# A fused linear-attention and mixer block: a lone row-tile pair for the last two tiles, and another order of all jobs

## The chip, the cores and the metric

The kernel runs on one core of one Trainium2 chip. The metric is the device time of one execution in microseconds (us), less is better. "TensorE" or PE is the matmul engine (PEld are its weight loads), DVE is VectorE, ACT is ScalarE, POOL is GpSimd, SP is SyncE, which here only issues DMAs.

## The reference

All tensors are bfloat16. x has 2048 tokens of 448 features; there are 16 heads of 28 features; w3 and w4 have 1792 hidden features.

```python
def _A_ref(x, wqkv, w_phi, wo):                 # linear attention
    q, k, v = heads(x @ wqkv)                   # 16 heads of 28
    pq, pk = q @ w_phi, k @ w_phi               # per head
    phi_q = concat(softmax(pq), softmax(-pq))   # 56 features a head
    phi_k = concat(softmax(pk), softmax(-pk))
    kv, z = phi_k^T v, sum_s phi_k
    o = (phi_q kv) / (phi_q z + 1e-6)
    return o.reshape(B, S, D) @ wo

def _B_ref(x, w1, w2, w3, w4):                  # token-shift mixer and MLP
    h = gelu(layernorm(x) @ w1)
    hs = concat(h[..., quarter i] shifted by (+1, -1, +2, -2)[i] tokens) @ w2
    x1 = x + hs
    return x1 + gelu(layernorm(x1) @ w3) @ w4

x = A_x
xn = layernorm(x)
return x + _A_ref(xn, A_wqkv, A_w_phi, A_wo) + _B_ref(xn, B_w1, B_w2, B_w3, B_w4)
```

## The kernel before

The 2048 tokens are 16 tiles of 128. A recorder (`Recorder`) takes every instruction in program order, works out which earlier ones it must wait for, and writes one instruction stream for each engine; each engine then runs its stream strictly in order. So the order in which the program calls its jobs is the order on every engine and on SP's DMA queue. Nearly all instructions are issued through helpers, which is why the profile's lines repeat: L204 is every matmul, L208 every transposing matmul, L212 every activation, L216 every elementwise operation of DVE and POOL, L219 a transposing DMA, L222 a plain DMA.

**Row pairs.** 448 rows of a contraction are held as four overlapping chunks of 128 rows that start at rows 0, 128, 192 and 320 (`load_lap`, `START`). Each chunk has a lower half (partitions 0 to 63, `LO`) and an upper half (64 to 127, `HI`). Rows 192 to 255 stand twice, so a product over 448 rows is seven halves. Two matmuls of 64 rows, one on each half and into different PSUM banks, run side by side in TensorE. For two tiles together 14 halves make seven such pairs. The recorder's rule: two matmuls that write the same PSUM bank from different halves are ordered by a semaphore wait (`solve`, lines 114 to 121). There are eight banks of 512 fp32 columns.

**First stage** (a list of jobs that `chain` plays, lines 969 to 990). It loads x, makes the layernorm statistics (`m` on DVE; the root as a power on POOL, `r`, or on ACT, `q`; the apply on DVE, `a`, or POOL, `p`), transposes each normalised tile into `xnT` (`XT` on TensorE with a copy out by ACT or DVE, or `XD` as a DMA on SP), computes V (`ZV`, copied out by `EV`), h = gelu(xn w1) (`ZH`, `ZW`, and `ZR` for the last 64 features; gelus by `EW` and `rest_out` on ACT), and folds w_phi into the q and k weights (`FO`). `HD` issues dummy matmuls into idle time. `chain` keeps one list of lower and one of upper halves and interleaves them: an upper half is issued `lag` columns after the lower half of the same bank. `h_shift` makes the token shift of h as six SBUF-to-SBUF DMAs per half of the tokens, `rest_T` transposes the gelu's last 64 features by DMA (tile `hR`, which shares its memory with `gT`, into `hRT`); both are on SP's queue.

**Second stage** (the list in `play`, lines 1055 to 1077). Its jobs: `k0`, `k1` and `q0`, `q1` (k and q features of two tiles in four and three row pairs of 448 columns, then two exponentials on ACT), `w0`, `w1_` (h w2 of two tiles, also four and three pairs; two adds on DVE bring the sum into `xn`, `w2_out`), `kn` (sums for k's softmax: a reduce and a reciprocal on DVE), `kx` (their product on POOL), `T` (transpose of q's exponentials by DMA), `K` (phi_k^T v of a tile into banks 6 and 7, eight pairs of 59 columns), `kc`, `kb` (kv to SBUF), `lo`, `sc` (statistics of the second norm), `A` (its apply, on POOL or DVE), `G` (its transpose by DMA into `gT`), `a`, `b` (w3 for 256 hidden features of 512 tokens, in four and three row pairs of 512 columns, then a gelu on ACT), `N` (numerator and denominator of a tile, six DVE operations, two on POOL, then the transpose `o_T` by DMA), `f` (four steps over a pair of tiles: w4 and wo into banks 4 and 5, then `fin_out` on DVE), `S` (store).

Which banks k, q, w2, V and h jobs use is fixed in `kq`, `wb`, `vb` and `gb`.

**The last two tiles.** Tiles 14 and 15 have no partner pair behind which their tail could hide, so they use 128-row matmuls: 14 of w4 and four of wo each. Since rows 192 to 255 stand in two chunks, `num_tile` fills 64 of the attention output's columns with zeros for these tiles. Tile 14 is one matmul group of 448 columns (`fin_full`), tile 15 is two groups of 256 and 192 columns (`fin_split`), each with its own add and store, the first store on ACT's queue and the last on SP's.

Of the kernel before, what the change touches and what calls it, by code (L numbers as in the profile page):

```python
# [18 lines left out]
class Recorder:  # L19
# [56 lines left out]
    def solve(self):  # L76
# [10 lines left out]
        for eng, fn, w, r, dma, tile in self.ops:  # L87
# [137 lines left out]
def bass_parallel_sum__linear_kernel_hedgehog__mixer_s_mlp__prompt_kernel(  # L225
# [17 lines left out]
    with es:  # L243
# [533 lines left out]
        def num_tile(i):  # L777
# [54 lines left out]
        def fin_bank(i):  # L832
            return (0 if i > 13 else 4) + i % 2

        def fin_full(i):
            g, j = divmod(i, 4)
            b = banks[fin_bank(i)]
            x_sum(i)
            for fc in range(FC):
                R.mm(b[:, 0:D], h3T[:, g % 2, fc, 128 * j:128 * j + 128], w4[:, fc, :], fc == 0, False)  # L840
            for kc in range(KC):
                R.mm(b[:, 0:D], oT[:, g % 2, kc, 128 * j:128 * j + 128], wo[:, kc, :], False, kc == KC - 1)

        def fin_split(i, cut):
            g, j = divmod(i, 4)
            x_sum(i)
            for n, (c0, c1) in enumerate(((0, cut), (cut, D))):
                b, c = banks[2 * n + 1], slice(c0, c1)
                for fc in range(FC):
                    R.mm(b[:, c], h3T[:, g % 2, fc, 128 * j:128 * j + 128], w4[:, fc, c], fc == 0, False)  # L850
                for kc in range(KC):
                    R.mm(b[:, c], oT[:, g % 2, kc, 128 * j:128 * j + 128], wo[:, kc, c], False, kc == KC - 1)
                R.ew(dve, "tensor_tensor", outb[:, i % 4, c], b[:, c], xs[:, i % 2, c], op=ALU.add)
                R.dma(out2d[128 * i:128 * i + 128, c], outb[:, i % 4, c], "SP" if n else "ACT")
# [59 lines left out]
        fb = {(1, 0): 3, (1, 2): 1, (0, 0): 3, (0, 2): 1}  # L914
# [4 lines left out]
        def L(*ops):  # L919
            return do(ln1, *ops)  # L920
# [39 lines left out]
        def HF(p, n):  # L960
# [4 lines left out]
        vb = {0: 2, 1: 5, 2: 4, 3: 6, 4: 5, 5: 4, 6: 6, 7: 7, 8: 0, 9: 7, 10: 1, 11: 4, 12: 7, 13: 0, 14: 5, 15: 3}  # L965
        gb = ((7, 2, 3), (1, 7, 0), (1, 0, 3), (4, 5, 6))
# [3 lines left out]
            HD(3, 3), HD(3, 3), do(load_wT, 0, (1, 2, 3)), L(("m", 0)), HD(6, 3), L(("r", 0, 1), ("a", 0), ("v", 1)),  # L970
            HD(2, 3), L(("m", 2), ("q", 1, 1), ("m", 3)), XT(0, 2, 1, "ACT"),
            L(("p", 1), ("q", 2, 1), ("a", 2), ("r", 3, 1), ("m", 5), ("m", 4), ("p", 3)), HD(4, 3), HD(5, 3),
            inside(3, ZV(0, EV(0, "ACT", 1)), XT(1, 5, 1, "ACT")), XT(2, 0, 1, "ACT"), ZV(1, EV(1, "ACT", 1)),
            L(("q", 5, 1)), inside(1, ZV(2, EV(2, "ACT", 1)), XT(3, 0, 1, "ACT")),
            L(("m", 6), ("q", 6, 1), ("p", 5), ("q", 4, 1), ("m", 7)), ZH(2, 0), L(("a", 6), ("a", 4)),
            inside(2, ZH(0, 0), XT(5, 0, 1, "ACT")), L(("r", 7, 1), ("m", 12), ("p", 7)), ZH(0, 1, EW(0, 0, 1)), ZH(1, 0),
            XT(6, 0, 1, "DVE"), XT(4, 5, 1, "ACT"), ZH(2, 1), L(("m", 13)), ZV(5, EV(5, "ACT", 1)), L(("r", 12, 1)),
            XT(7, 0, 1, "DVE"), L(("m", 14), ("p", 12), ("r", 13, 1)), ZV(4, EV(4, "ACT", 1)), ZV(3, EV(3, "ACT", 1)),
            L(("m", 15), ("r", 14, 1), ("m", 8)), ZH(1, 1, EW(0, 1, 2)), ZW(1, 1, EW(1, 1, 1)), ZW(1, 2, EW(1, 2, 1)),
            L(("r", 15, 1)), XT(12, 4, 1, "ACT"), ZV(6, EV(6, "ACT", 1)), L(("a", 14), ("a", 15), ("a", 13)), do(load_w2),  # L980
            XT(14, 2, 2, "2"), inside(2, ZW(1, 0, EW(1, 0, 1)), XT(13, 4, 1, "DVE")), L(("r", 8, 1), ("p", 8)),
            ZV(7, EV(7, "ACT", 1)), L(("m", 10)), ZW(3, 0, EW(3, 0, 1)), L(("m", 11)), ZV(15, EV(15, "ACT", 1)),
            L(("r", 10, 1)), XD(8), L(("p", 10), ("m", 9), ("r", 11, 1)), XD(10), ZV(14, EV(14, "ACT", 1)), do(phi_blocks),
            ZV(13, EV(13, "ACT", 1)), L(("a", 11)), XD(11), L(("r", 9, 1)), FO(1, 2, 0), do(load_w3, 0),
            inside(2, ZW(3, 2, EW(3, 2, 1)), FO(1, 2, 1)), inside(2, ZV(12, EV(12, "ACT", 1)), FO(1, 0, 0)), FO(1, 0, 1),
            do(h_shift, 0), ZW(3, 1, EW(3, 1, 1)), inside(1, ZV(8, EV(8, "ACT", 1)), FO(0, 2, 0)), L(("p", 9)),
            XT(9, 3, 1, "DVE"), FO(0, 2, 1), ZR(0, 6, (rest_out, 0, 6), (rest_T, 0)), ZV(9, EV(9, "ACT", 1)), do(late_3),
            FO(0, 0, 0), ZV(10, EV(10, "ACT", 1)), inside(1, ZR(1, 2, (rest_out, 1, 2)), FO(0, 0, 1)), ZW(2, 1, EW(2, 1, 1)),
            ZV(11, EV(11, "ACT", 1)), ZW(2, 2, EW(2, 2, 1)), ZW(2, 0, EW(2, 0, 1)), HF(2, 0), HF(0, 0), do(load_w4),
            do(kv_picks), do(h_shift, 1), HF(1, 0), do(kv_ones), do(rest_T, 1), HF(0, 1), HF(1, 1), HF(2, 1)], 500, 2)  # L990

        on_dve = (7, 8, 12, 13, 15)
# [58 lines left out]
        def wo_in(eng="SP"):  # L1051
# [4 lines left out]
            (k0, 1), (kn, 0), (w0, 2), (k1, 1), (k0, 2), (T, 0), (kx, 0), (lo, 1), (w1_, 2), (kn, 1), (k1, 2), (q0, 1),  # L1056
            (q0, 2), (q1, 1), (kn, 2), (q1, 2), (w0, 4), (k0, 3), (w1_, 4), (T, 1), (k1, 3), (kx, 1), (q0, 3), (k0, 4),
            (q1, 3), (k1, 4), (w0, 6), (T, 2), (kn, 3), (lo, 2), (q0, 4), (w1_, 6), (kx, 2), (kx, 3), (T, 4), (K, 0), (K, 3),
            (q1, 4), (lo, 0), (K, 5), (T, 3), (T, 7), (T, 6), (lo, 3), (sc, 0), (k0, 5), (K, 4), (A, 1), (kn, 4), (A, 3),
            (k1, 5), (q0, 5), (T, 5), (A, 2), (A, 0), (load_w3, 1), (G, 1), (w0, 8), (G, 3), (q1, 5), (k0, 6), (w1_, 8),  # L1060
            (k1, 6), (K, 2), (q0, 6), (kn, 5), (w0, 10), (q1, 6), (w1_, 10), (G, 2), (lo, 7), (kx, 4), (lo, 5), (lo, 4),
            (G, 0), (k0, 7), (lo, 6), (K, 7), (kn, 6), (kx, 5), (K, 6), (k1, 7), (q0, 7), (w0, 12), (q1, 7), (w1_, 12),
            (sc, 4), (a, 0), (A, 6), (A, 4), (kx, 6), (G, 6), (kn, 7), (K, 1), (K, 10), (b, 0), (a, 1), (K, 9), (lo, 10),
            (K, 11), (wo_in,), (K, 8), (b, 1), (w0, 14), (G, 4), (a, 2), (a, 3), (b, 2), (b, 3), (A, 7), (lo, 11), (A, 5),
            (lo, 8), (kx, 7), (w1_, 14), (G, 5), (K, 13), (a, 4), (G, 7), (T, 12), (lo, 9), (a, 5), (b, 4), (K, 12), (T, 14),
            (K, 15), (sc, 8), (K, 14), (kc,), (b, 5), (lo, 12), (a, 6), (kb,), (A, 10), (b, 6), (a, 7), (N, 1), (b, 7),
            (f, 1, 0), (N, 0), (T, 10), (A, 11), (G, 10), (a, 8), (a, 9), (A, 8), (T, 11), (G, 8), (A, 9), (b, 8), (b, 9),
# [13 lines left out]
        fin_split(15, 256)  # L1081
# [30 lines left out]
```

## Time and profile before

| | us |
|---|---|
| median of 3 runs | 173.25 |
| the three runs | 173.14, 173.25, 176.32 |
| the profiled execution's own time | 172.24 |
| its span, first to last instruction | 170.5 |
| TensorE busy in the span | 166.2 |
| DVE, POOL, ACT busy | 108.4, 92.2, 83.9 |

"Busy" is the time in which at least one instruction of the engine runs. The span is one execution; the time around it is not in the trace. In the timeline rows, the columns are the start and the length in us, the engine, the line, the operation, what it writes and reads, the shapes, the number of instructions merged, and in brackets the idle time before it with what ended it. Where matmuls are merged, the length includes the last one's way through the array, so a pitch is read from start to start. The granted TensorE clock was full throughout.

### The profile page before, as it was taken

The page shows a single profiled execution, that of the slowest core. Times are in us where ns is not written, and L with a number is a line of the kernel's source. Part 1 is how long each engine was busy: PE and PEld are TensorE (multiplying, and loading weights), DVE is VectorE, ACT ScalarE, POOL GpSimd, SP SyncE. Part 2 cuts the span into 40 slices and gives each one's busy share as a digit, 9 for nine tenths or more (in the row PEclk, how much of TensorE's full clock was granted, in tenths as well). Part 3 has the DMA queues.
Part 4 walks back from the last instruction along what each step waited for, and adds up shares of the span by engine and source line. Part 5 has one row for each costly group of instructions (what it writes and reads, how often), then busy time and mean ns, then how long its engine had stood idle before and what let it go on. Part 6 is the DMA issues. An engine that isn't in the chain of part 4 may idle for free.

```text
span 170.5 us, 5420 instructions
## 1 busy us (share of the span) xinstructions
PE 166.2 (97%) x2351; PEld 96.3 (56%) x2351; DVE 108.4 (64%) x246; ACT 83.9 (49%) x114; POOL 92.2 (54%) x128
## 2 busy tenths in 40 slices
PE   8899999999999999999999999999999999999994
PEld 7576789655555555554554554554545555545463
DVE  3798865249999799967678933757407552425621
ACT  5789866879999879357242240421304222404000
POOL 6588590005799999992585272094420754023740
PEclk9999999999999999999999999999999999999999
DMA  5995677999599940569037949945440113021141
GB/s 153 359 207 99 150 84 210 190 351 171 118 134 191 257 98 0 142 126 94 0 64 136 113 96 168 139 105 78 92 115 0 35 31 112 4 58 31 31 117 48
DMA packets 51111, 20.07 MB, mean 118 GB/s; under 512 B 42256, under 2 KB 50384, under 8 KB 51088
## 3 DMA queue, kind: packets, MB, share of 16 engines
q1 hardware_dynamic: 49968, 18.86, 58.1%
q10 hardware_dynamic: 1120, 0.87, 1.5%
q8 instruction: 18, 0.29, 0.8%
q14 instruction: 5, 0.04, 0.1%
HBM read 7.14 MB, written 1.84 MB: 53 GB/s over the span
## 4 chain that ended last, share of the span: by engine, by line
PE 88%; DMA 5%; SPq 3%; DVE 1%; POOL 1%; issue 1%
PE banks L204 87%; SPq L222 3%; DMA hRT<-gT 2%; DMA xtok<-in_A_x_dram 2%; PE banks L208 1%; DVE st L216 1%; POOL rs L216 0%; POOL xn L216 0%; DVE xnT L216 0%; DVE mv L216 0%; DVE vaug L216 0%
## 5 line engine op out<-in xcount | busy, mean ns | idle before, releaser
L212 ACT ACTIVATE phik<-banks 128x1024 bf16<-128x1024 f32 (+1 forms) x44 | 41.8, 985 | 61.1 <-PE banks L204 61.0
L204 PE MATMUL banks<-gT,w 64*128 64x512 bf16 x392 | 48.0, 376 | 0.0
L216 DVE TENSOR_TENSOR vaug<-banks,vaug 128x464 f32<-128x464 f32 (+3 forms) x65 | 32.7, 513 | 23.1 <-PE banks L204 21.4
L204 PE MATMUL banks<-w,phik 64*128 64x448 bf16 (+3 forms) x434 | 45.2, 343 | 0.0
L216 POOL TENSOR_TENSOR xnT<-vaug 128x280 bf16<-128x280 f32 (+1 forms) x32 | 18.1, 586 | 45.9 <-DVE vaug L216 45.9
L204 PEld LDWEIGHTS banks<-w,phik 64*128 64x128 bf16 (+1 forms) x434 | 22.8, 94 | 19.1 <-issue 0.4
L204 PE MATMUL banks<-wv,xnT 64*128 64x448 bf16 (+3 forms) x222 | 32.4, 346 | 0.2
L734 POOL TENSOR_TENSOR phik<-phik,rks 128x1792 bf16<-128x1792 bf16 x8 | 25.6, 3212 | 9.1 <-DVE rks L216 8.8
L204 PEld LDWEIGHTS banks<-gT,w 64*128 64x128 bf16 x392 | 18.0, 94 | 18.4 <-ACT phik L212 0.7
L204 PEld LDWEIGHTS banks<-wv,xnT 64*128 64x128 bf16 (+1 forms) x222 | 14.0, 94 | 8.1 <-ACT xnT L212 0.8
L216 POOL TENSOR_TENSOR vaug<-xn,xtok 128x448 f32<-128x448 bf16 x16 | 16.2, 1031 | 1.1 <-DVE vaug L216 1.1
L216 DVE TENSOR_REDUCE ksum<-phik 128x64 f32<-128x1792 bf16 x8 | 16.0, 1996 | 0.2 <-ACT phik L212 0.2
L204 PE MATMUL banks<-xnT,w 64*128 64x512 bf16 (+1 forms) x105 | 16.0, 334 | 0.0
L212 ACT ACTIVATE hi<-banks 128x896 bf16<-128x896 f32 x16 | 13.7, 919 | 2.3 <-PE banks L204 2.3
L204 PE MATMUL banks<-wpk,xnT 64*128 64x448 bf16 x112 | 14.2, 349 | 0.0
L204 PE MATMUL banks<-wpq,xnT 64*128 64x448 bf16 x112 | 13.7, 349 | 0.0
L216 DVE RECIPROCAL vaug<-banks 128x16 f32<-128x16 f32 x16 | 4.1, 254 | 15.2 <-PE banks L204 15.2
L216 POOL TENSOR_TENSOR rs<-mv,mhalf 128x1 f32<-128x1 f32 (+1 forms) x15 | 10.4, 697 | 5.3 <-DVE mv L216 5.2
L204 PE MATMUL banks<-w,hT 64*128 64x448 bf16 x96 | 12.8, 349 | 0.0
L216 DVE TENSOR_TENSOR xn<-banks,xn 128x512 bf16<-128x512 f32 (+1 forms) x16 | 9.0, 601 | 3.6 <-PE banks L204 3.6
L216 DVE BATCH_NORM_STATS2 st<-xn 128x6 f32<-128x448 bf16 x16 | 9.4, 590 | 0.0
L216 DVE BATCH_NORM_STATS2 st<-xtok 128x6 f32<-128x448 bf16 x15 | 9.0, 601 | 0.4 <-DMA xtok<-in_A_x_dram 0.4
(71 smaller groups left out, 167.2 us busy)
## 6 DMA issues: line engine op xcount, KB each, us to landing
w<-in_B_w_dram SPq DMA_DIRECT2D x2, 896.0 KB, 5.7
out_dram<-vaug SPq DMA_DIRECT2D x15, 112.0 KB, 1.9
w<-in_B_w_dram SPq DMA_DIRECT2D x1, 1568.0 KB, 9.3
xtok<-in_A_x_dram SPq DMA_DIRECT2D x2, 448.0 KB, 6.3
wv<-in_A_wo_dram SPq DMA_DIRECT2D x2, 224.0 KB, 3.8
xtok<-in_A_x_dram SPq DMA_DIRECT2D x3, 112.0 KB, 3.9
xtok<-in_A_x_dram ACTq DMA_DIRECT2D x3, 112.0 KB, 4.1
w<-in_B_w_dram SPq DMA_DIRECT2D x1, 336.0 KB, 4.4
```

Of the source, the lines that this page charges most:

```text
L204: self.op("PE", lambda e: e.matmul(out, lhsT, rhs, start=start, stop=stop, skip_group_check=True), [out], [lhsT, rhs], tile=self._tile(lhsT))
L208: self.op("PE", lambda e: e.transpose(out, in_, ident), [out], [in_, ident], tile=self._tile(in_))
L212: self.op("ACT", lambda e: e.activation(out, in_, func, **kw), [out], [in_] + aps)
L216: self.op(eng, lambda e: getattr(e, name)(out, *args, **kw), [out], aps)
L222: self.op(eng, lambda e: e.dma_start(out, in_), [out], [in_], dma=True)
L734: R.op(pool, lambda e: e.tensor_tensor(ph, ph, wide, op=ALU.mult), [ph], [ph, wide, *after])
```

## The change

It does these things.

1. The recorder's rule is widened: a wait is also set where the same half wrote the same bank before a change between 64-row and 128-row form.
2. `fin_tails` is new. Chunk 1's lower half (rows 128 to 191) for tile 14 and chunk 2's upper half (rows 256 to 319) for tile 15 are issued as a pair of 64 rows that opens the three output groups; the full matmuls that follow then need only three chunks a tile. The zero fill goes.
3. Tile 15's groups become 320 and 128 columns.
4. Tile 14's second norm apply moves from POOL to DVE (`on_dve` has six tiles now).
5. The first stage's list, its banks (`vb`, `gb`, `fb`), `lag` (500 to 300) and `even` (2 to 1) are others. Tile 8 is transposed on TensorE and no longer by DMA, tile 3's root goes to ACT, V of tiles 3 and 8 is copied out by DVE, and several of the copies out of `XT` change between ACT and DVE.
6. The second stage's list has the same 259 entries in another order. Banks of k, q, w2 and w3 jobs stay.

```diff
-                        if lo != tile[0]:
+                        if lo != tile[0] or m != mode[1]:
...
-            if i >= NT - 2:
-                c0 = 192 + 64 * (i % 2)
-                R.ew(pool, "memset", o_tok[:, i % 4, c0:c0 + 64], 0.0)
...
+        def fin_tails(i, cut):
+            x_sum(i)
+            g, j = divmod(i, 4)
+            c = 128 * j
+            R.mm(banks[0][:, 0:D], oT[0:64, g % 2, 1, c:c + 128], wo[0:64, 1, :], True, False)
+            for n, (c0, c1) in enumerate(((0, cut), (cut, D))):
+                R.mm(banks[2 * n + 1][:, c0:c1], oT[64:128, g % 2, 2, c + 128:c + 256], wo[64:128, 2, c0:c1], True, False)
+
+        def fin_steps(b, i, c, kcs):
+            g, j = divmod(i, 4)
+            s = slice(128 * j, 128 * j + 128)
+            for fc in range(FC):
+                R.mm(b[:, c], h3T[:, g % 2, fc, s], w4[:, fc, c], False, False)
+            for kc in kcs:
+                R.mm(b[:, c], oT[:, g % 2, kc, s], wo[:, kc, c], False, kc == KC - 1)
+
         def fin_full(i):
-            g, j = divmod(i, 4)
-            b = banks[fin_bank(i)]
-            x_sum(i)
-            for fc in range(FC):
...
+            fin_steps(banks[0], i, slice(0, D), (0, 2, 3))
...
+                fin_steps(b, i, c, (0, 1, 3))
...
-            L(("m", 0)), HD(6, 3), L(("r", 0, 1), ("a", 0), ("v", 1)),
-            HD(2, 3), L(("m", 2), ("q", 1, 1), ("m", 3)), XT(0, 2, 1, "ACT"),
-            L(("p", 1), ("q", 2, 1), ("a", 2), ("r", 3, 1), ("m", 5), ("m", 4), ("p", 3)), HD(4, 3), HD(5, 3),
...
-            L(("r", 10, 1)), XD(8), L(("p", 10), ("m", 9), ("r", 11, 1)), XD(10), ZV(14, EV(14, "ACT", 1)), do(phi_blocks),
...
+            HD(1, 3), L(("m", 0), ("r", 0, 1), ("a", 0)), HD(2, 3), L(("v", 1), ("q", 1, 1), ("m", 2)), HD(0, 3),
+            XT(0, 6, 1, "ACT"), L(("p", 1), ("m", 3), ("q", 2, 1)), HD(1, 3), L(("q", 3, 1)), HD(3, 3),
+            L(("a", 2), ("m", 5)), HD(3, 3), inside(2, ZV(0, EV(0, "ACT", 1)), XT(1, 0, 1, "ACT")), L(("m", 4)),
+            XT(2, 6, 1, "ACT"), ZV(1, EV(1, "ACT", 1)), L(("m", 6), ("p", 3), ("q", 5, 1)), XT(3, 0, 1, "ACT"),
...
+            FO(1, 0, 1), L(("p", 9)), XT(8, 1, 1, "ACT"), ... inside(2, ZV(8, EV(8, "DVE", 1)), FO(0, 0, 0)), do(h_shift, 0),
...
-        on_dve = (7, 8, 12, 13, 15)
+        on_dve = (7, 8, 12, 13, 14, 15)
...
-            (G, 0), (k0, 7), (lo, 6), (K, 7), (kn, 6), (kx, 5), (K, 6), (k1, 7), (q0, 7), (w0, 12), (q1, 7), (w1_, 12),
-            (sc, 4), (a, 0), (A, 6), (A, 4), (kx, 6), (G, 6), (kn, 7), (K, 1), (K, 10), (b, 0), (a, 1), (K, 9), (lo, 10),
-            (K, 11), (wo_in,), (K, 8), (b, 1), (w0, 14), ...
+            (lo, 6), (G, 1), (K, 5), (kx, 5), (lo, 7), (K, 2), (k1, 7), (sc, 4), (w0, 12), (A, 5), (q0, 7), (A, 4),
+            (w1_, 12), (G, 4), (q1, 7), (K, 4), (a, 0), (kn, 6), (w0, 14), (b, 0), (a, 1), ...
...
-            (f, 3, 5), (a, 26), (f, 4, 5), (S, 10), (N, 14), (b, 27), (b, 26), (f, 1, 6), (f, 2, 6), (N, 15), (f, 3, 6),
-            (S, 11), (S, 12), (S, 13)])
+            (f, 4, 5), (a, 26), (S, 11), (S, 10), (N, 15), (S, 9), (a, 27), (b, 26), (b, 27), (f, 1, 6), (f, 2, 6),
+            (f, 3, 6), (S, 12), (S, 13)])
+        fin_tails(14, 320)
         fin_full(14)
         fin_out(14)
         store(14)
-        fin_split(15, 256)
+        fin_split(15, 320)
```

More of the change, by code (lines that the diff above doesn't have):

```diff
@@ L848, in fin_split @@
                 b, c = banks[2 * n + 1], slice(c0, c1)
[L849 to L852, printed above, removed]
+                fin_steps(b, i, c, (0, 1, 3))
                 R.ew(dve, "tensor_tensor", outb[:, i % 4, c], b[:, c], xs[:, i % 2, c], op=ALU.add)
@@ L912, in ln1 @@
                     ln1_apply(pool if op == "p" else dve, *n)
-        fb = {(1, 0): 3, (1, 2): 1, (0, 0): 3, (0, 2): 1}
+        fb = {(1, 0): 4, (1, 2): 1, (0, 0): 3, (0, 2): 3}
         def do(f, *args):
@@ L963, in HF @@
             return "half", halves_of(*head[p][n], n == 0), then
[L965 to L966 removed]
+        vb = {0: 5, 1: 3, 2: 4, 3: 6, 4: 5, 5: 4, 6: 6, 7: 5, 8: 0, 9: 1, 10: 7, 11: 5, 12: 7, 13: 0, 14: 2, 15: 7}
+        gb = ((7, 2, 3), (0, 7, 0), (0, 3, 1), (3, 5, 6))
         spin(30)
@@ L975, in bass_parallel_sum__linear_kernel_hedgehog__mixer_s_mlp__prompt_kernel @@
[L975 to L979, printed above, removed]
@@ L985, in bass_parallel_sum__linear_kernel_hedgehog__mixer_s_mlp__prompt_kernel @@
[L985 to L989, printed above, removed]
@@ new lines, in bass_parallel_sum__linear_kernel_hedgehog__mixer_s_mlp__prompt_kernel @@
+            L(("m", 7), ("q", 4, 1), ("p", 5)), ZH(1, 0), ZV(2, EV(2, "ACT", 1)), do(load_wT, 0, (1, 2, 3)),
+            L(("q", 6, 1), ("p", 4), ("a", 6)), ZH(0, 0), L(("m", 13)), XT(5, 0, 1, "ACT"), L(("r", 7, 1)),
+            ZH(0, 1, EW(0, 0, 1)), ZH(2, 0), L(("m", 12)), XT(4, 5, 1, "ACT"), XT(6, 0, 1, "ACT"), L(("m", 14), ("p", 7)),
+            ZH(2, 1), L(("r", 13, 1)), ZV(5, EV(5, "ACT", 1)), L(("r", 12, 1)), ZV(3, EV(3, "DVE", 1)), XT(7, 0, 1, "DVE"),
+            L(("r", 14, 1)), ZV(4, EV(4, "ACT", 1)), L(("m", 15)), ZH(1, 1, EW(0, 1, 2)), ZW(1, 2, EW(1, 2, 1)), do(load_w2),
@@ new lines, in bass_parallel_sum__linear_kernel_hedgehog__mixer_s_mlp__prompt_kernel @@
+            ZW(1, 1, EW(1, 1, 1)), L(("p", 13), ("a", 12), ("a", 14), ("r", 15, 1), ("a", 15)), XT(12, 4, 1, "DVE"),
+            L(("m", 10), ("r", 10, 1), ("m", 11)), ZV(6, EV(6, "ACT", 1)), L(("r", 11, 1), ("p", 10), ("m", 8)),
+            XT(14, 1, 2, "ACT"), XT(13, 3, 1, "DVE"), ZV(7, EV(7, "ACT", 1)), do(phi_blocks), L(("m", 9)),
+            ZW(1, 0, EW(1, 0, 1)), L(("r", 8, 1)), ZV(14, EV(14, "ACT", 1)), XD(10), L(("a", 8), ("a", 11), ("r", 9, 1)),
+            XD(11), ZV(15, EV(15, "ACT", 1)), do(load_w3, 0), ZW(3, 0, EW(3, 0, 1)),
@@ new lines, in bass_parallel_sum__linear_kernel_hedgehog__mixer_s_mlp__prompt_kernel @@
+            inside(2, ZV(13, EV(13, "ACT", 1)), FO(1, 0, 0)), FO(1, 0, 1), L(("p", 9)), XT(8, 1, 1, "ACT"),
+            ZW(3, 2, EW(3, 2, 1)), inside(2, ZV(12, EV(12, "ACT", 1)), FO(1, 2, 0)), do(late_3), XT(9, 3, 1, "DVE"),
+            FO(1, 2, 1), ZW(3, 1, EW(3, 1, 1)), inside(2, ZV(8, EV(8, "DVE", 1)), FO(0, 0, 0)), do(h_shift, 0), FO(0, 0, 1),
+            ZR(0, 6, (rest_out, 0, 6), (rest_T, 0)), ZV(9, EV(9, "ACT", 1)),
+            inside(2, ZR(1, 2, (rest_out, 1, 2)), FO(0, 2, 0)), ZW(2, 0, EW(2, 0, 1)), ZV(10, EV(10, "ACT", 1)), FO(0, 2, 1),
@@ L993, in bass_parallel_sum__linear_kernel_hedgehog__mixer_s_mlp__prompt_kernel @@
+            ZV(11, EV(11, "ACT", 1)), ZW(2, 2, EW(2, 2, 1)), ZW(2, 1, EW(2, 1, 1)), HF(0, 0), HF(2, 0), HF(1, 0),
+            do(kv_picks), do(load_w4), do(rest_T, 1), do(kv_ones), do(h_shift, 1), HF(0, 1), HF(1, 1), HF(2, 1)], 300, 1)
+        on_dve = (7, 8, 12, 13, 14, 15)
         kp = [phi_pair(wpk, 2 * n, kq[n][0]) for n in range(8)]
```

49 lines of the change are left out of this document (19 added, 30 removed).

## The prediction

> **What bounds the kernel now.** I read the page's busy shares first, then the busy time by stage, then who made TensorE wait, and only then the stretches that the new order touches.
>
> ```profile
> span 170.5 us, 5420 instructions
> PE 166.2 (97%) x2351; PEld 96.3 (56%) x2351; DVE 108.4 (64%) x246; ACT 83.9 (49%) x114; POOL 92.2 (54%) x128
> ```
> ```profile
> 9.12:34.24 25.12, 24.86 (x480) 19.33 (x480) 16.92 (x45) 20.50 (x38) 13.66 (x25) 1.00 0.85 152
> 34.24:68.00 33.76, 33.76 (x485) 18.61 (x486) 29.97 (x44) 29.26 (x35) 26.08 (x17) 1.00 0.85 166
> 68.00:161.04 93.04, 93.04 (x1246) 47.82 (x1238) 53.71 (x138) 28.42 (x30) 44.31 (x58) 1.00 0.46 81
> ```
> ```profile
> PE banks L204 <- PEq L1097: 0.8, 1, 0.8
> PE banks L208 <- DVE xn L216: 0.3, 1, 0.3
> PE banks L204 <- DMA hRT<-gT: 0.3, 1, 0.3
> PE banks L208 <- POOL xn L216: 0.2, 1, 0.2
> ```
> The columns of the middle fence are the window, its length, and the busy time (with instruction counts) of PE, PEld, DVE, ACT and POOL, then clock, DMA share and GB/s. TensorE is the bound: 97% of the span, and 100% from 34.24 us to the last tiles. Waits of TensorE add up to 1.6 us, of which 0.8 us lies ahead of its first instruction. A busy TensorE could still run at half pace, so I check its pitch:
>
> ```profile
> 157.72 2.82 PE L204 MATMUL banks<-w,phik 64*128 64x448 bf16 x28
> 160.38 0.73 PE L204 MATMUL banks<-wv,xnT 64*128 64x448 bf16 x6
> 161.04 2.82 PE L204 MATMUL banks<-w,phik 128*128 128x448 bf16 x14
> 163.70 0.92 PE L204 MATMUL banks<-wv,xnT 128*128 128x448 bf16 x4
> 164.46 1.69 PE L204 MATMUL banks<-w,phik 128*128 128x256 bf16 x14
> 165.99 0.60 PE L204 MATMUL banks<-wv,xnT 128*128 128x256 bf16 x4
> 166.43 1.32 PE L204 MATMUL banks<-w,phik 128*128 128x192 bf16 x14
> 167.58 0.49 PE L204 MATMUL banks<-wv,xnT 128*128 128x192 bf16 x4
> ```
> From start to start, 14 pairs of 64 rows take 160.38 - 157.72 = 2.66 us, 0.190 us a pair. The 128-row matmuls of tile 14 take (163.70 - 161.04) / 14 = 0.190 us as well. So a row pair really runs as one. An order can only remove waits, and there is little left to remove; 2% of the median of 173.25 us, about what a measurement of this kernel can tell from no change, is 3.5 us.
>
> The profiled execution took 172.24 us, its span 170.5 and 1.74 us around it. It lies 1.0 us under the median of the three runs, so I sum changes against 172.24 and carry the difference over.
>
> **Part 1, the last two tiles.** Pitch of the other widths, from the fence above: 256 columns (165.99 - 164.46) / 14 = 0.109 us, 192 columns (167.58 - 166.43) / 14 = 0.082 us. The step of 64 columns is 0.027 us. Before: 18 x (0.190 + 0.109 + 0.082) = 6.86 us. After: one row pair (0.190) and 17 matmuls of each width. I take 320 columns at 0.136 us and 128 at 0.055 us by the same step, so 0.19 + 17 x (0.190 + 0.136 + 0.055) = 6.67 us: **-0.19 us**. The unknown is whether a 128-row matmul of 128 columns can follow its weights at 0.055 us. If it stayed at the 192-column pitch of 0.082, 17 x 0.027 = 0.46 us come back. For the lower value speaks this row:
>
> ```profile
> 65.86 0.62 PE L204 MATMUL banks<-vaug,phik 64*128 64x59 bf16 x32
> 66.31 1.67 PE L204 MATMUL banks<-gT,w 64*128 64x512 bf16 x14
> ```
> Thirty-two weight loads and matmuls take 66.31 - 65.86 = 0.45 us, 28 ns a pair, so loading does not need 82 ns there. I take 0.055 and keep 0.46 us for the range.
>
> The Trainium skill ("TensorE: Matmul & The Clock Gate", section Back-to-back issue gap) speaks against this: a sustained stream of weight loads and matmuls is said to need about 81 ns each at N = 128, and 131 ns at N = 512. By its 81 ns the tail would come out some 0.3 us longer than before instead of shorter. For its second figure this trace disagrees: 448 columns alone took 190 ns.
>
> The pair comes in 64-row form, the rest in 128-row form, as the old switch did: its last pair began at 160.38 + 2 x 0.19 = 160.76 us, the first 128-row matmul at 161.04, 0.09 us over the pitch. The changed rule for waits adds one: tile 14's first full matmul goes to bank 0, where the pair has just written, and must wait for its end. It costs between 0 (the old drain covers it) and 0.17 us (a whole 0.36 us matmul instead of a pitch of 0.19); I take 0.1. That matmul is the head of TensorE's queue, and everything to the end stands behind it.
>
> ```profile
> 166.63 0.42 DVE L216 TENSOR_TENSOR vaug<-banks,vaug 128x256 bf16<-128x256 f32 x1 [1.34 <-PE banks L204]
> 168.11 0.36 DVE L216 TENSOR_TENSOR vaug<-banks,vaug 128x192 bf16<-128x192 f32 x1 [1.06 <-PE banks L204]
> out_dram<-vaug ACTq DMA_DIRECT2D x1, 64.0 KB, 1.6
> out_dram<-vaug SPq DMA_DIRECT2D x1, 48.0 KB, 1.5
> ```
> 64 columns fewer make the last add 0.06 us shorter; its store is 1.5 us whatever I do. The other group's add starts 17 x 0.055 = 0.94 us ahead of the end, takes 0.48 us and lands 1.6 us later, 1.1 us behind the end; the last group lands 0.3 + 1.5 = 1.8 us behind it, so it still sets the end. The two zero fills that go were GpSimd work under TensorE's 2.66 us of pairs: nothing. The pair needs both attention tiles ahead of w4 instead of behind it, but N(15) now has ten pairs of 512 columns and the 35 pairs of tiles 12 and 13 behind it, 10 x 0.217 + 35 x 0.190 = 8.8 us (0.217 is 512 columns at the pitch of 448). Before, its matmuls ended by 157.72 and its tile was used at 165.99, 8.3 us later and without a wait. The cover holds. Sum of the part: -0.19 + 0.1 - 0.06 = **-0.15 us**, from -0.35 to +0.4.
>
> **Part 2, the transposes of the first stage.** Here the old order has its one real stall:
>
> ```profile
> 21.02 4.81 SPq L219 DMA_TRANSPOSE xnT<-xn  x3
> ...
> 26.50 3.75 SPq L222 DMA_DIRECT2D hT<-hT  x6
> 30.29 1.50 SPq L219 DMA_TRANSPOSE hRT<-gT  x1
> 30.29 3.90 DMA hRT<-gT
> 28.11 0.60 ACT L212 ACTIVATE gT<-banks 128x512 bf16<-128x512 f32 x1 [0.67 <-PE banks L204]
> 33.62 0.35 PE L204 MATMUL banks<-w,hT 64*128 64x448 bf16 x1
> 34.24 0.36 PE L204 MATMUL banks<-w,hRT 64*128 64x448 bf16 x1 [0.27 <-DMA hRT<-gT]
> ```
> SP's queue issues without a pause: three transposes of x, the load of w3, six copies for the shift, then the transpose of the gelu's last 64 rows. Its input was done at 28.71 us; it went out at 30.29 and landed at 34.19. TensorE should have gone on at 33.62 + 0.19 = 33.81 and went on at 34.24: 0.43 us lost. The change turns tile 8's transpose (1.26 to 1.3 us of SP) into a TensorE one. All else in front of it on SP keeps its order, so the hRT transpose leaves at about 29.0 us, still behind its input, and lands at 32.9, ahead of need: **-0.43 us**. What is late next is the shift's copies, which move up by as much.
>
> ```profile
> L208 PE MATMUL banks<-ident,xn 64*128 64x64 bf16 x104 | 3.9, 191 | 0.5 <-DVE xn L216 0.3 <-POOL xn L216 0.2
> L212 ACT ACTIVATE xnT<-banks 128x512 bf16<-128x512 bf16 x7 | 4.2, 596 | 1.1 <-PE banks L208 1.1
> 10.00:15.00 5.00, 5.00 (x97) 4.15 (x96) 4.70 (x15) 4.81 (x11) 4.15 (x9) 1.00 1.13 121
> ```
> The price: eight transposing matmuls at 3.9 / 104 = 0.037 us of busy time each, 0.30 us at most, and 8 x 0.014 = 0.11 us by the 59-column row; +0.15 us, near the lower, because busy time counts overlaps of the chain. Its copy and those of other tiles move to ACT, 2.5 x 0.60 = 1.5 us more there, and two V copies leave it for DVE: less than 1.5 us in a stage where ACT is busy 20.50 of 25.12 us. That is nothing, unless it falls near 10 to 15 us, where ACT is busy 4.81 of 5 (rival 3). Part 2: **-0.28 us**.
>
> **Part 3, the first tiles.**
>
> ```profile
> 7.00 0.20 DVE L216 BATCH_NORM_AGGREGATE mv<-st 128x2 f32<-128x9 f32 x1
> 7.08 0.60 ACT L212 ACTIVATE xnT<-banks 128x512 bf16<-128x512 bf16 x1 [0.38 <-PE banks L208]
> 7.74 1.15 PE L204 MATMUL banks<-wv,xnT 64*128 64x448 bf16 x7
> 9.12 0.29 PE L208 MATMUL banks<-ident,xn 64*128 64x64 bf16 x8 [0.23 <-POOL xn L216]
> ```
> Tile 3's root goes from GpSimd's power to ACT. Its transpose, which waited 0.23 us at 9.12, can come earlier: -0.23. But the root sits on ACT ahead of tile 1's copy and needs the statistics that end at 7.20. Queued behind it, the copy leaves at about 7.47 instead of 7.08, and tile 1's V matmuls behind that: +0.39 if nothing else fills TensorE. I take **+0.1 us**, from -0.3 to +0.5. The dummy matmuls are only redistributed around tile 0's transpose, into idle time.
>
> **Part 4, the order from 34 us on.** All 259 jobs are the same; their TensorE work is the same. Where the order can cost is a bank taken before it is read out, in the stage where DVE is busy 29.97 of 33.76 us.
>
> ```profile
> L216 DVE TENSOR_REDUCE ksum<-phik 128x64 f32<-128x1792 bf16 x7 | 14.0, 1995 | 0.2 <-ACT phik L212 0.2
> L216 DVE RECIPROCAL rks<-ksum 128x64 f32<-128x64 f32 x7 | 3.9, 553 | 0.2
> 60.91 1.09 DVE L216 TENSOR_TENSOR xn<-banks,xn 128x512 bf16<-128x512 f32 x2
> ```
> The tightest place is (w0, 14): it takes banks 4 and 5 after w2_out(12). Between the two stand now 3 pairs, K(4) and a(0), that is 3 x 0.190 + 16 x 0.014 + 4 x 0.217 = 1.66 us; before, two a, two b and five K jobs stood there, 14 x 0.217 + 80 x 0.014 = 4.2 us. The read-out needs 1.09 us and a matmul's 0.35 us of latency: 0.2 us to spare. But in DVE's queue the reduce of kn(6) now stands behind that read-out and no longer ahead of it, so DVE should be there in time: **0**, from -0.3 (other small gaps) to +2.5 us (one reduce and reciprocal in front). The sixth norm apply on DVE lies in the stage where DVE is busy 53.71 of 93.04 us: nothing.
>
> **Sum:** -0.15 - 0.28 + 0.1 + 0 = -0.33 us: 171.9 for the profiled execution, 172.9 us against the median.
>
> **Rivals.** (1) *The wait is replaced.* The hRT transpose still comes too late, because the shift's copies ahead of it on SP wait for a gelu that now comes later. For it: SP works strictly in order. Against: the gelu input was ready 1.58 us ahead of the issue. The -0.43 goes: 173.35 us. (2) *Weight loads bound the 128-column group*, +0.46: 173.4 us. Against it is the 28 ns row; for it, only that those loads fill half the rows. (3) *ACT holds up the transposes*: an added copy (0.60) falls on the path near 10 to 15 us, and tile 1's delay of 0.39 is not given back: 172.9 + 0.6 + 0.3 = 173.8 us. (4) *DVE becomes the bound*, slower than before: at (w0, 14), or the w2 read-outs ahead of it, a reduce stands in front while TensorE wants the bank. It decides once DVE is more than 0.2 us behind there; then the price is a reduce and its reciprocal, 2.0 + 0.55 - 0.2 = 2.3 us: 175.2 us, and twice that if it strikes w0(8) too, 177.5. DVE's 89% in the stage speaks for it, the reduce's new place against it.
>
> **Chances.** Forecast 0.46, rival (1) 0.13, (2) 0.11, (3) 0.08, (4) 0.13 and its double 0.06 more; 0.03 that gaps which no view shows close too and the gain passes 3.5 us, for which all waits of 1.6 us are not enough. Faster by over 2%: 0.03. Slower by over 2% (above 176.7 us): the double and a share of rival (4), 0.09. Within: 0.88. The range goes from 172.0 (parts 1, 3 and 4 at their better ends) to 175.3, rival (4).
>
> **What would show it.** Right: no wait of TensorE for hRT; an hRT transpose issued near 29 us; TensorE 100% busy from 34 us on; 128-column matmuls starting 55 ns apart; one gap of at most 0.2 us after the lone pair. Wrong: those matmuls 80 ns apart; a TensorE wait for DVE or ACT between 34 and 70 us; V matmuls of tile 1 later than 8.2 us with nothing in between; a last store that is not the 128-column one.

## The result and the profile after

| | us |
|---|---|
| median after, 22 runs | 171.69 (171.17 to 173.68) |
| median before, 22 runs beside them | 173.56 (171.81 to 176.32) |
| ratio after / before | 0.9916 (0.9894 to 0.9938) |
| the profiled execution after, its span | 171.45, 169.7 |

The ratio leaves out disturbed runs, so it is not quite the quotient of the two medians. It is a gain of 0.84%, 1.46 us of 173.56 (1.08 to 1.84), well inside the 2% that I had called no change. I had forecast 0.33 us. So "within 2%" was right, the sign was right, and the size was four times too small: by the ratio 173.25 becomes 171.8, just below the low end of my range (172.0).

From the page of the kernel after, the span, the busy row and the chain that ended last:

```profile
span 169.7 us, 5428 instructions
...
PE 166.1 (98%) x2359; PEld 95.0 (56%) x2359; DVE 109.2 (64%) x247; ACT 83.7 (49%) x114; POOL 90.6 (53%) x124
...
PE 94%; DMA 2%; DVE 1%; SPq 0%; ACT 0%; issue 0%
```

The last row is the share of the chain that ended last, by engine. TensorE is busy for as long as before (166.1 us against 166.2). Who made TensorE wait in the kernel after (total, times, longest), and its busy time by stage (the columns are those of the prediction's table):

```profile
PE banks L204 <- PEq L1101: 0.8, 1, 0.8
PE banks L204 <- ACT xnT L212: 0.2, 1, 0.2
```
```profile
9.12:34.24 25.12, 25.12 (x489) 19.58 (x484) 17.38 (x45) 20.83 (x38) 13.45 (x24) 1.00 0.89 158
34.24:68.00 33.76, 33.76 (x491) 18.02 (x489) 31.06 (x45) 29.12 (x35) 26.50 (x17) 1.00 0.85 158
```

The waits for the hRT transpose, DVE and POOL have gone; from 9.12 us to 68 us TensorE is never idle. The first matmul that reads hRT, which began at 34.24 us before, begins here at

```profile
33.37 0.35 PE L204 MATMUL banks<-w,hRT 64*128 64x448 bf16 x1
```

From there TensorE needs 134.0 us to its end, and before it needed 133.8. So in these two traces the whole difference on TensorE lies ahead of that matmul, in the first stage. SP's queue in the kernel after (start, length, what it issues) shows the mechanism of part 2 as foretold, with two transposes of x instead of three and the hRT transpose issued at 29.30 us (I had said about 29.0) instead of 30.29:

```profile
21.47 2.59 SPq L219 DMA_TRANSPOSE xnT<-xn  x2
24.11 1.36 SPq L222 DMA_DIRECT2D w<-in_B_w_dram  x1
25.50 3.75 SPq L222 DMA_DIRECT2D hT<-hT  x6
29.30 1.75 SPq L219 DMA_TRANSPOSE hRT<-gT  x1
```

The tail of the kernel after, TensorE's timeline and then DVE's last add:

```profile
159.75 0.92 PE L204 MATMUL banks<-wv,xnT 64*128 64x448 bf16 x9
160.73 2.82 PE L204 MATMUL banks<-w,phik 128*128 128x448 bf16 x14
163.38 0.73 PE L204 MATMUL banks<-wv,xnT 128*128 128x448 bf16 x3
163.95 2.06 PE L204 MATMUL banks<-w,phik 128*128 128x320 bf16 x14
165.85 0.57 PE L204 MATMUL banks<-wv,xnT 128*128 128x320 bf16 x3
166.26 0.94 PE L204 MATMUL banks<-w,phik 128*128 128x128 bf16 x14
167.04 0.33 PE L204 MATMUL banks<-wv,xnT 128*128 128x128 bf16 x3
```
```profile
167.41 0.29 DVE L216 TENSOR_TENSOR vaug<-banks,vaug 128x128 bf16<-128x128 f32 x1 [0.46 <-PE banks L204]
```

The first row holds the last three pairs of wo and the lone pair. The 128-column matmuls start (167.04 - 166.26) / 14 = 0.056 us apart, the 320-column ones (165.85 - 163.95) / 14 = 0.136.

### The profile page after: what moved, and what is told of

The parts are those of the page before. It is cut to its first block, busy times and chain, and to the rows that moved or that the text cites. A ratio compares the mean times of both kernels' runs of the same rounds, so it can differ in the third digit from the quotient of the medians.

```text
span 169.7 us, 5428 instructions
## 1 busy us (share of the span) xinstructions
PE 166.1 (98%) x2359; PEld 95.0 (56%) x2359; DVE 109.2 (64%) x247; ACT 83.7 (49%) x114; POOL 90.6 (53%) x124
## 3 DMA queue, kind: packets, MB, share of 16 engines
HBM read 7.14 MB, written 1.84 MB: 53 GB/s over the span
## 4 chain that ended last, share of the span: by engine, by line
PE 94%; DMA 2%; DVE 1%; SPq 0%; ACT 0%; issue 0%
PE banks L204 93%; DMA xtok<-in_A_x_dram 2%; PE banks L208 1%; DVE st L216 1%; SPq L222 0%; ACT xnT L212 0%; DVE mv L216 0%; DVE vaug L216 0%; ACT rs L212 0%
## 5 line engine op out<-in xcount | busy, mean ns | idle before, releaser
L204 PE MATMUL banks<-wv,xnT 64*128 64x448 bf16 (+3 forms) x222 | 33.5, 346 | 0.3 <-ACT xnT L212 0.2
L204 PEld LDWEIGHTS banks<-w,phik 64*128 64x128 bf16 (+1 forms) x434 | 22.3, 94 | 19.8 <-PE banks L204 0.8
L734 POOL TENSOR_TENSOR phik<-phik,rks 128x1792 bf16<-128x1792 bf16 x8 | 25.6, 3211 | 8.5 <-DVE rks L216 8.3
L204 PE MATMUL banks<-xnT,w 64*128 64x512 bf16 (+1 forms) x105 | 18.5, 334 | 0.0
L216 POOL TENSOR_TENSOR rs<-mv,mhalf 128x1 f32<-128x1 f32 (+1 forms) x14 | 9.7, 692 | 6.4 <-DVE mv L216 6.3
```

What stands on the lines that cost most here:

```text
L204: self.op("PE", lambda e: e.matmul(out, lhsT, rhs, start=start, stop=stop, skip_group_check=True), [out], [lhsT, rhs], tile=self._tile(lhsT))
L216: self.op(eng, lambda e: getattr(e, name)(out, *args, **kw), [out], aps)
L734: R.op(pool, lambda e: e.tensor_tensor(ph, ph, wide, op=ALU.mult), [ph], [ph, wide, *after])
```

## The experiments

Twelve kernels ran, in three groups of four, each group beside the kernel before on one chip; the medians of before were 173.71, 173.67 and 173.57 us. Where I give a ratio in us, it is of 173.6.

**1. The first stage alone.** Before, with the new first list, its banks and its lag; the old second list and the old tail.

```diff
-        vb = {0: 2, 1: 5, 2: 4, 3: 6, ...}
-        gb = ((7, 2, 3), (1, 7, 0), (1, 0, 3), (4, 5, 6))
+        vb = {0: 5, 1: 3, 2: 4, 3: 6, ...}
+        gb = ((7, 2, 3), (0, 7, 0), (0, 3, 1), (3, 5, 6))
...
-            ... HF(0, 1), HF(1, 1), HF(2, 1)], 500, 2)
+            ... HF(0, 1), HF(1, 1), HF(2, 1)], 300, 1)
```

> The kernel before with the first stage's list, banks and lag of the kernel after; second list and tail as before. Measured for the whole change: -1.5 us, where the prediction's sum was -0.33. Theory A (the gain sits in the first stage: no late hRT transpose, tile 3 earlier, and both cost more in an ordinary execution than in the one profiled): -1.0 to -1.4 us. Theory B (the gain sits in the order of the second stage): -0.2 to -0.4 us, what the prediction's parts 2 and 3 give. Theory C (it sits in the tail): the same, -0.2 to -0.4.

Measured: 171.68 us, ratio 0.9912 (0.9884 to 0.9941), span 169.6. By the centres, the whole gain lies in the first stage.

**2. The second list alone.** Before, with the new list of the second stage and the sixth norm apply on DVE.

```diff
-        on_dve = (7, 8, 12, 13, 15)
+        on_dve = (7, 8, 12, 13, 14, 15)
...
-            (k0, 1), (kn, 0), (w0, 2), (k1, 1), (k0, 2), (T, 0), ...
+            (k0, 1), (w0, 2), (k1, 1), (lo, 1), (k0, 2), (kn, 0), ...
```

> The kernel before with the second stage's list of the kernel after (and its six norm applies on VectorE); first stage and tail as before. Theory A: within 0.2 us of before, and its trace shows the hRT wait again. Theory B: -0.8 to -1.2 us. Theory C: within 0.2 us.

Measured: 174.27 us, 1.0044 (0.9996 to 1.0092): no gain, and no loss that stands clear of 1. Its profile held the first surprise. From TensorE's waits and its timeline, a wait that the profile of before does not have at all:

```profile
PE banks L204 <- DMA xnT<-xn: 1.8, 1, 1.8
```
```profile
26.33 0.35 PE L204 MATMUL banks<-wv,xnT 64*128 64x448 bf16 x1 [1.79 <-DMA xnT<-xn]
```

The wait ends at 26.33 us; the list that was edited begins at about 34. The DMA waited for is tile 8's transpose, in this kernel's chain of waits (start, length):

```profile
21.50 4.70 DMA xnT<-xn
```

In the profiled execution of before the same DMA, issued at 21.02 us, was in time for V(8). Both kernels have the same list of first-stage jobs, so the profiled execution of before may have been a lucky one. The next runs are about that.

**3. The tail alone.** Before, with the lone pair, the 320 and 128 columns and the rule for waits; (N, 14) and (N, 15) stand further ahead, behind (f, 2, 5) and (f, 4, 5), since the pair needs them.

```diff
+        fin_tails(14, 320)
...
-        fin_split(15, 256)
+        fin_split(15, 320)
```

> The kernel before with the lone row pair, groups of 320 and 128 columns and the widened wait rule; its own two lists, except that N(14) and N(15) are called one and two steps earlier, so that tile 15's attention output lies ready for the pair (behind f(2,5) and f(4,5)). The prediction's part 1: -0.15 us. Theory A: -0.1 to -0.2. Theory B: the same. Theory C: -0.8 or more. Rival 2 of the prediction (weights bound the 128-column group): +0.3 us, starts 80 ns apart instead of 55.

Measured: 173.60 us, 1.0003 (0.9965 to 1.0041), span 170.6; times cannot resolve the part. Traces can: in every profile with the old tail the last pair of wo starts 7.31 us ahead of TensorE's end and 9.74 to 9.77 us ahead of the span's end; with the new tail, here and in the kernel after, it is 7.24, and 9.56 to 9.59 us. That is 0.18 us less, 0.07 of it on TensorE and the rest behind it.

**4 and 5. Tile 8's transpose, in two other ways.** Before, with it on TensorE; and before, with it still a DMA, but ahead of the load of w2 on SP.

```diff
-            L(("r", 10, 1)), XD(8), L(("p", 10), ...), XD(10), ZV(14, EV(14, "ACT", 1)), do(phi_blocks),
+            L(("r", 10, 1)), L(("p", 10), ...), XD(10), ZV(14, EV(14, "ACT", 1)), XT(8, 6, 1, "ACT"), do(phi_blocks),
```

> The kernel before, where tile 8's transpose is a TensorE one with a copy on ACT and no longer a DMA on SP; nothing else changed. Prediction's part 2: hRT is issued 1.3 us earlier, no wait for it, -0.28 us. Theory A: more in the median, -0.4 to -0.9 us, because the wait for hRT differs between executions. Theory B: -0.1 to -0.3.

Measured: 172.74 us, 0.9978 (0.9937 to 1.0019). By the ratio that is 0.4 us, with 1 inside its interval, so it does not tell part 2's -0.28 from theory A. TensorE no longer waits for hRT, and ten of the twelve runs lie between 172.46 and 173.07 us.

```diff
-            ... L(("a", 14), ("a", 15), ("a", 13)), do(load_w2),
+            ... L(("a", 14), ("a", 15), ("a", 13)),
...
-            L(("r", 10, 1)), XD(8), L(("p", 10), ...
+            L(("r", 10, 1)), XD(8), do(load_w2), L(("p", 10), ...
```

> The kernel before with one change of order on SP's queue: the three loads of w2 are issued behind tile 8's transposing DMA and no longer ahead of it, so that it leaves about 2.8 us earlier. Theory D (tile 8's transpose, when it is in flight at the instruction load of about 23.5 us, is held 2 us, and V of tile 8 waits 1.8 us for it; the profiled execution of before just escaped): no such wait in any execution, median 172.4 to 172.9 us, as with tile 8 on TensorE, and a narrow spread. Theory E (tile 8's transpose only takes SP's time from hRT): 173.3 to 173.7, since SP's total work is unchanged.

Measured: 173.02 us, 0.9959 (0.9931 to 0.9988). Nothing moves to TensorE here and the transpose of hRT still makes it wait (0.2 us), yet about 0.7 us go. That is under the 173.3 us at which theory E began, so more than SP's time counts, and the kernel before seems to lose time at tile 8's DMA in its usual execution, although its profile shows no such wait. Theory D is not borne out in full either: the median misses its range (172.4 to 172.9), and the runs are not close together (172.00 to 174.35, half of them over 173.1). The loads of w2 moved back too, and no run separates their share.

**6. Tile 3's root on ACT alone**, in before:

```diff
-            L(("p", 1), ("q", 2, 1), ("a", 2), ("r", 3, 1), ...
+            L(("p", 1), ("q", 2, 1), ("a", 2), ("q", 3, 1), ...
```

> The kernel before with tile 3's root on ACT in place of GpSimd's power; nothing else changed. Prediction's part 3: between -0.3 and +0.5 us. Theory A (first stage): the first 10 us of the profiles lose 0.4 to 0.7 us less in the kernel after, and if the root is what does it: -0.4 to -0.7 us. If it is the order of the jobs around it: 0 to -0.2.

Measured: 173.44 us, 0.9973 (0.9943 to 1.0003). The centre is a gain of 0.5 us; alone it does not settle the sign. Its profile, of an execution of 175.63 us, shows tile 8's wait again: the DMA was issued at 21.85 us and landed 4.6 us later, and V(8) waited 2.0 us for it.

**7. Edits 4 and 6 together.**

> The kernel before with both edits: tile 8's transpose on TensorE and tile 3's root on ACT. Both together against the whole first stage (171.7 us): if the two are all that counts in it, 171.6 to 172.0; if its order, banks and lag count too, 172.2 to 172.7.

Measured: 172.69 us, 0.9955 (0.9930 to 0.9980). That is about half of the gain of the first stage (0.9912); the other half needs the rest of the new order. The two ran in different groups, but their runs do not overlap: all twelve here took 172.26 us or more, all twelve of experiment 1 172.26 or less. TensorE by stage, and the first matmul on hRT, first here, then in experiment 1:

```profile
9.12:34.24 25.12, 25.12 (x479) 18.93 (x476) 16.73 (x43) 20.43 (x40) 13.47 (x24) 1.00 0.90 149
34.32 0.35 PE L204 MATMUL banks<-w,hRT 64*128 64x448 bf16 x1
```
```profile
9.12:34.24 25.12, 25.12 (x489) 19.67 (x484) 17.26 (x45) 20.82 (x38) 13.45 (x24) 1.00 0.80 158
33.35 0.35 PE L204 MATMUL banks<-w,hRT 64*128 64x448 bf16 x1
```

Both keep TensorE busy for all of this stage, and in both 588 matmuls with the same sum of columns stand ahead of hRT, yet experiment 1 gets there 0.97 us sooner. On their pages TensorE's 2359 matmuls are busy for 167.0 us here and 165.5 there. So this half of the gain is not idle time: another order gets the same matmuls done in less busy time. How is not shown; a half that runs without a partner at its side would count as busy too.

**8. The kernel after with the old tail.**

```diff
-        fin_tails(14, 320)
...
-        fin_split(15, 320)
+        fin_split(15, 256)
```

> The kernel after with the tail of before: no lone pair, four wo chunks a tile, groups of 256 and 192 columns, zero fill back; both lists as after. Prediction's part 1: 0.15 us slower than the kernel after, 171.8 to 171.9. If the lone pair's wait eats its gain: the same time, 171.6 to 171.7.

Measured: 172.28 us, 0.9937 (0.9906 to 0.9968), against 0.9916 for the kernel after, and above both expected times. The difference has the sign of the tail's 0.18 us and is not resolved. The profile of this run is of an execution of 173.48 us and holds an idle time of TensorE of 1.0 us, near 28 us, for which it shows no wait; its cause is open.

**9. The kernel after with tile 8 transposed by DMA again**, between tiles 10 and 11 on SP.

```diff
-            ... XD(10), L(("a", 8), ("a", 11), ("r", 9, 1)),
+            ... XD(10), L(("a", 8), ("a", 11), ("r", 9, 1)), XD(8),
...
-            ... FO(1, 0, 1), L(("p", 9)), XT(8, 1, 1, "ACT"),
+            ... FO(1, 0, 1), L(("p", 9)),
```

> The kernel after with one edit undone: tile 8 is transposed by a DMA on SP again, issued between tile 10's and tile 11's, and no longer on TensorE. Theory D (a transpose in flight at the instruction load near 24 us is held, and V of tile 8 waits): issued near 22.8 us, landed near 26.5, V of tile 8 wants it near 24 to 25 us: a wait of 1 to 2 us in most executions, 172.8 to 173.5 us. Prediction's part 2 (SP's time only): hRT 1.3 us later, +0.3 us, 172.0.

Measured: 174.59 us, 1.0078 (1.0036 to 1.0120): slower than before, and above every time expected. Against 0.9916 it is 1.6%, 2.8 us, for one transpose. The row of TensorE's timeline, and then the row of its chain of waits that released it (start, length):

```profile
27.16 0.54 PE L204 MATMUL banks<-wv,xnT 64*128 64x448 bf16 x3 [2.66 <-DMA xnT<-xn]
```
```profile
23.05 3.97 DMA xnT<-xn
```

The DMA lands at 27.02 us and V(8) goes on at 27.16. The wait is about as long as the loss. Not all of it is a slow DMA: it was issued 2 us later than in before, and with the 2.5 us that it took there it would have landed at 25.6, about 1 us after TensorE was ready for V(8) (27.16 - 2.66 = 24.50). The other 1.5 us are its longer way. What happens in that time shows in the DMA view of 23 to 27 us, in 40 slices of 0.1 us: the busy share of the DMA engines in tenths, what they moved, and the queue of instruction loads (packets, MB, share). First this kernel, then the kernel before:

```profile
DMA  4879999996392799999999000000000010059999
GB/s 128 165 188 251 240 242 209 160 113 44 49 213 56 146 236 218 200 202 177 72 36 21 0 0 8 8 10 10 8 10 10 10 13 0 13 113 210 210 187 228
q8 instruction: 1, 0.02, 2.0%
```
```profile
DMA  1008006999999970000000000000399999820000
GB/s 8 0 0 164 0 15 128 207 207 207 205 179 70 8 0 0 0 5 8 8 10 10 8 10 10 8 8 0 67 184 195 225 228 200 177 37 0 0 0 0
q8 instruction: 1, 0.02, 2.2%
```

In both, all transfers nearly stand still for 1.3 to 1.5 us: from 25.2 to 26.5 us here, from 24.3 to 25.8 in before. In both an instruction load falls into the window; single packets of the trace put its start at 24.12 and 23.34 us, and the load's packet itself takes 1.30 and 1.42 us. In before, tile 8's transpose was already there. Its row of the DMA view (in the window from 20.9 to 21.2 us; the last number is the time from issue to landing), and TensorE's timeline of before, the first matmul of V(8):

```profile
xnT<-xn SPq DMA_TRANSPOSE x1, 2.5
```
```profile
24.16 0.35 PE L204 MATMUL banks<-wv,xnT 64*128 64x448 bf16 x1
```

Issued at 21.02 us, it landed at 23.5: 0.8 us ahead of the standstill and 0.6 us ahead of its use. In the profile of the tail alone it was issued at 21.17 us and came through as well; issued at 21.50 us (experiment 2), 21.85 (experiment 6) and 23.05 (here) it was caught, and V(8) waited 1.8, 2.0 and 2.7 us. In experiment 2 the whole wait is due to that: 2.8 us after its issue, at 24.3, it would still have been in time for TensorE, which was ready at 24.54. The times fit: the two executions that escaped took 172.24 and 172.37 us, near the quickest of their kernels (medians 173.56 and 173.60), and the one of experiment 2, which was caught, took 174.03 (median 174.27).

**10. The kernel after with tile 3's root on POOL again.**

```diff
-            ... HD(1, 3), L(("q", 3, 1)), HD(3, 3),
+            ... HD(1, 3), L(("r", 3, 1)), HD(3, 3),
```

> The kernel after with tile 3's root back on GpSimd. By the prediction's part 3 the root's move was worth -0.1 us against (it cost): 171.6. If it was worth the 0.3 to 0.4 us that the first 10 us of the two profiles differ by: 172.0 to 172.1.

Measured: 172.25 us, 0.9943 (0.9909 to 0.9978), span 170.6; 0.5 us above the kernel after by the centres, and above both expected times. First ACT's and TensorE's timeline of this kernel, then those of the kernel after:

```profile
7.22 0.60 ACT L212 ACTIVATE xnT<-banks 128x512 bf16<-128x512 bf16 x1
```
```profile
8.10 0.73 PE L204 MATMUL banks<-wv,xnT 64*128 64x448 bf16 x5
9.54 0.29 PE L208 MATMUL banks<-ident,xn 64*128 64x64 bf16 x8 [0.71 <-POOL xn L216]
```
```profile
7.24 0.20 ACT L212 ACTIVATE rs<-mv 128x1 f32<-128x1 f32 x1 [0.59 <-DVE mv L216]
7.34 1.13 ACT L212 ACTIVATE xnT<-banks 128x512 bf16<-128x512 bf16 x2
```
```profile
7.98 0.74 PE L204 MATMUL banks<-wv,xnT 64*128 64x448 bf16 x5
8.64 0.29 PE L208 MATMUL banks<-ident,xn 64*128 64x64 bf16 x8
```

The root on ACT delays the copies behind it by 0.12 us (7.22 to 7.34), and tile 3's transpose comes 0.9 us earlier and without its wait of 0.71 us.

**11 and 12. Two more edits of the kernel after**: the old lag, and the lone pair one step earlier, so that three pairs of wo lie between it and the matmul that waits for its bank.

```diff
-            ... HF(0, 1), HF(1, 1), HF(2, 1)], 300, 1)
+            ... HF(0, 1), HF(1, 1), HF(2, 1)], 500, 2)
```

> The kernel after with the first stage's lag and even of before (500 and 2 instead of 300 and 1): upper halves are issued later behind the lower halves of their bank, and one more job at the end keeps its halves in the old split. If the closer interleaving is what the first stage gains beside tile 8 (0.7 to 1.0 us): 172.2 to 172.7. If its order of jobs and banks is: 171.6 to 171.8.

Measured: 171.71 us, 0.9916 (0.9876 to 0.9956), span 169.8: the times show no effect of the lag, and in the trace TensorE reaches hRT at 33.54 us, 0.17 later than in the kernel after.

```diff
-            (f, 3, 6), (S, 12), (S, 13)])
-        fin_tails(14, 320)
+            (f, 3, 6), (fin_tails, 14, 320), (f, 4, 6), (S, 12), (S, 13)])
+        x_sum(14)
```

> The kernel after with the lone row pair called ahead of the last seven-half step of tiles 12 and 13 and no longer behind it (tile 14's x sum stays where it was). The wait of the first full matmul for the pair's end, about 0.19 us over the pitch in the trace of after, of which 0.09 us belong to the change of form, goes: TensorE's end comes 0.10 us sooner after the last pair, 171.6 us, within the noise of the times but visible in the trace.

Measured: 171.74 us, 0.9906 (0.9871 to 0.9942), span 170.0. From TensorE's timeline:

```profile
160.18 0.92 PE L204 MATMUL banks<-wv,xnT 64*128 64x448 bf16 x9
161.04 0.36 PE L204 MATMUL banks<-w,phik 128*128 128x448 bf16 x1
```

The same nine matmuls now take 161.04 - 160.18 = 0.86 us to the first 128-row matmul, against 160.73 - 159.75 = 0.98: the wait for the bank cost 0.12 us. No time tells this kernel from the kernel after, and neither is shown to be the better.

## Why the prediction was right, and where its size was not

**What bounds the kernel** was right, TensorE, but the sentence that an order can only remove waits was not: experiments 1 and 7 differ by 1.5 us of busy time with the same matmuls. A TensorE that is 100% busy still left room for the order, and the sum had no term for it.

**Part 1 (-0.15 us)** was right in sum and in its terms: 0.18 us less in the traces, the 128-column pitch 0.056 us against 0.055, 320 columns at 0.136, the last add 0.07 us shorter against 0.06. The nine matmuls of the last row-pair group should take 4 x 0.19 = 0.76 us; the gap behind them is 0.98 - 0.76 = 0.22 us, a hair over the 0.19 (0.09 and 0.1) of my working; its bank wait was 0.12. Rival (2) is refuted by the 0.056. So is, for this case, the 81 ns at N = 128 that the Trainium skill ("TensorE: Matmul & The Clock Gate", section Back-to-back issue gap) gives for a sustained stream; the formula that the section keeps for an isolated matmul, N / 2.4 + 2.5 ns, gives 55.8 ns and agrees with it.

**Part 2 (-0.28 us)** was too small in size. Its mechanism worked as described: tile 8 left SP, hRT went out 1 us earlier, its wait is gone, rival (1) did not come. But the term was sized by the one wait that the profiled execution showed, 0.43 us for hRT. By the runs above, what tile 8's DMA usually costs is its own late landing, which that execution had escaped. I had noted that it lay 1.0 us under the median and carried the difference over unchanged, as if the same time were lost everywhere; it was a clue that the usual execution has a stall which this trace does not show. Experiment 5 removes about 0.7 us without touching hRT's cause, and experiment 9, whose transpose is also issued later, brings 2.8 us back. Experiment 4, the edit by itself, gives 0.4 us with a wide interval, so how much too small the term was is not settled. The times agree: two of the 22 runs of before are under 172.1 us, and 18 of the 22 after.

**Part 3 (+0.1 us)** had the wrong sign. I charged tile 1's V matmuls with 0.39 us for a root ahead of their copy. They did come later than before (7.98 against 7.74 us), yet with the root on POOL in the new order they come later still (8.10): the root costs that copy 0.12 us, and tile 3's transpose gains 0.9. Undoing it costs 0.5 us at the centre, with intervals that overlap, and TensorE's waits in the trace grow by 0.9 us.

**Part 4 (0)** was right: TensorE is busy 33.76 of 33.76 us with DVE at 31.06, its time from hRT to the end stayed within 0.2 us, so neither (w0, 14) nor rival (4) struck, and the first stage alone is as quick as the whole change. Rival (3) did not come either.

**The sum.** Parts 2 and 3 together stood for -0.18 us; their two edits gave 0.8 us (experiment 7). The rest of the first stage's order, its banks and its lag had no term, that is, nothing, and gave about as much again. That the sign came out right owes something to luck: most of the gain came from places that the forecast priced too low, with the wrong sign, or not at all.

**What stays open.** The two named edits together reach 0.9955, the first stage 0.9912: some 0.75 us are due to the rest of its order. The traces place them in TensorE's busy time ahead of hRT (experiment 7), and no run here says to which job or bank they belong, except that the lag has little part in it (experiment 11). My copy of tile 8 in bank 6 may itself cost a part. Why half of the runs of experiment 5 are still over 173.1 us is not known. That the standstill is caused by the instruction load, and not merely timed with it, was argued from when they occur; no run moved the load.

## What to carry to other kernels

Look at the spread and at where the profiled execution lies in it before sizing a term: if the trace is quicker than the median, a stall may be missing from it, and it is to be sought at transfers that land less than a microsecond ahead of their use (here 0.6 us). An engine that is busy all the time can still get through the same instructions sooner in another order; compare when it reaches the same instruction, and not only its idle time. In a kernel bound by TensorE a transpose of at most 0.3 us on TensorE can be cheaper than a DMA that costs nothing as long as it is on time. A root moved to another queue is worth what it takes off the tile that waits, and what it puts in front of others may be far less than the whole instruction's length.

## What the runs showed of the hardware

Transposing DMAs are held up more often around instruction loads than elsewhere. A packet of 256 bytes, as a transpose moves them, takes 0.018 us in the median of every profile. In the 14 profiles, with 252 instruction loads, there are 131 moments at which such packets take 0.85 to 2.2 us (long packets that start less than 0.5 us apart are one moment); 94 of them begin within 1.2 us after the start of a load. These stretches make up 18 x 1.2 / 170 = 13% of the time, 10% of all packets of 256 bytes start in them, and they hold 72% of the moments; of the other 37 I know no cause. Tile 8's transpose landed 2.5 to 2.8 us after its issue when it was clear of one (before, the tail alone), and 4.0 to 4.7 us after it when it was not (experiments 2, 5, 6 and 9; in experiment 5 a load at 19.64 us caught it, early enough to do no harm). The page of the kernel after counts these loads (packets, MB, share of 16 engines):

```profile
q8 instruction: 18, 0.29, 0.8%
```

That is 16 KB a load, one in about 9 us. The Trainium skill ("Runtime: NRT & Kernel Launch", section Instruction fetch mechanics) says that a sequencer fetches its instructions itself, in blocks of 16 KiB, over a DMA queue of its own, and that the cost is mostly hidden. The block size agrees with this row; that it is hidden does not hold for a transpose in flight beside it, if the load is the cause: V(8) waited 1.8 us in experiment 2.
